# An SSM convolution beside a mixer MLP: half of the taps transposed by DMA, weights placed in halves, output sums by DMA, a new order

## The chip, the cores and the metric

The kernel runs on one core of a Trainium2 chip. A core has five engines that run their own instruction streams and meet through semaphores: TensorE (PE) for matmuls, VectorE (DVE) for elementwise work, ScalarE (ACT) for activations and for moving PSUM to SBUF, GpSimd (POOL), and SyncE (SP), which here only issues DMAs. PSUM is used as four pairs of banks. The metric is the device time of one execution in microseconds.

## The reference

The input `x` (called `A_q`) has 2048 tokens of 640 features. Two branches are mixed by a gate per token.

```python
g = sigmoid((x * gate_w).sum(-1))
# branch a: causal depthwise conv of k (4 taps), times v, long convolution, times q
kv = k_shift * v
y  = irfft(rfft(kv_pad) * rfft(ssm_k_pad))[:2048] + kv * ssm_D
a  = q * y                                  # q is x
# branch b: token mixing and an MLP
h  = gelu(layernorm(x) @ w1)                # 640 x 640
x1 = x + shift_tokens(h) @ w2               # four feature groups shifted by 1,-1,2,-2
b  = x1 + gelu(layernorm(x1) @ w3) @ w4     # 640 -> 1536 -> 640
out = g * a + (1 - g) * b
```

## The kernel before

Token `t` sits at partition p of half c with t = 1024 c + 8 p + rho, so that work goes by rho = 0 to 7 and c = 0, 1. One large SBUF arena holds every tensor at fixed offsets; pieces are used again for other tensors when they are free.

**Branch b.** LN1 takes statistics of each row (`bn_group`, L800 and L802 on DVE), a power of -0.5 on POOL (`ln_finish`, L794), and normalizes on DVE (`normal`, L626, tag xn). PE transposes the rows (L839), ACT copies them to `XT` (L652, tag xTe). `mm1` (L876) makes h; its 160-column groups leave a fifth tile whose rows travel by small DMAs on POOL's queue (L916, tag tail) to their shifted places in `HT`. mm2 (L983) adds onto x, which ACT has put into PSUM first (`seed`, L966). LN2 comes from sums that ACT accumulates (the eviction's accumulator and a Square pass, L638); its normalized rows go through a DMA transpose on SP's queue (L1006, tag xT). mm3 (L1026) and mm4 (L1044) are the MLP, in four stages of 512 tokens each. The weights w3 and w4 are loaded on POOL's queue once the places of w1, w2 and of the kv scratch are free.

**Branch a.** The convolution is done by transforms as matmuls over 128 frequencies, in two halves of 320 features each. `kv` is computed on DVE in four blocks (L621). The taps `ssm_k` arrive with features on partitions and must be transposed: 80 transposes on PE (L773) and eight evictions on ACT (L779) fill `TAP`, whose first row then gets ssm_D added on DVE. `forward` (L1075) makes the spectra of the taps ("h") and of kv ("k") for a half, which ACT evicts into slots; `unit` (butterfly, window, pointwise, fold) is all DVE; `inverse` (L1198) brings the product back, ACT scales it by the gate, DVE multiplies by q and adds onto the scaled b in `X` (tag fin), and SP's queue writes the output (L1227).

**The gate.** The gate weights are loaded as a column (L711); PE multiplies them with `XT` (L933), the result is corrected by LN1's statistics, and ACT makes tanh of it.

**Order.** Nothing is ordered by the source text. Every operation is a node with its reads and writes; a planner (`_forward`) plays the program with estimated costs and due times and emits each engine's instructions in the order in which it started them. Ties go by a table of ranks (`PRIO`). So a queue is strictly in order: an instruction that waits holds all that stand behind it, and this includes the DMA issues on SP and POOL. `FILL` groups of small matmuls (L717) with no use but to keep PE busy are put wherever the planner finds PE idle.

The core of the tap transposes before:

```python
SSM[:, c, 1024 * a + rho:1024 * a + 1024:8], ident))   # 5 per t, 16 t
o = TAP[:, :, 2 * m:2 * m + 2, :].rearrange("p h t d -> p t h d")
```

Of the kernel before, what the change touches and what calls it, by code (L numbers as in the profile page):

```python
# [88 lines left out]
class Prog:  # L89
# [82 lines left out]
    def dma(self, queue, fn, r=(), w=(), nbytes=0, cost=0.4, kind="dma", group=None, final=False, tag="", land=None):  # L172
# [27 lines left out]
    def _forward(self):  # L200
# [38 lines left out]
        while left:  # L239
# [42 lines left out]
            if n.array:  # L282
# [5 lines left out]
                if not warm:  # L288
                    cost += n.array
# [4 lines left out]
            free[e] = t + cost  # L294
            if n.kind == "c":
                n.end = t + cost
            elif n.kind == "dma":
                link = max(link, t + 1.2) + n.bytes / self.RATE
                n.end = link + n.land
            elif n.kind == "acc":  # L300
                alink = max(alink, t + 1.2) + n.bytes / 150e3
                n.end = alink + 1.6
            elif n.kind == "side":
                slink = max(slink, t + 1.0) + 0.2
                n.end = slink + (4.0 if link > t else 1.0)
            else:
                xlink = max(xlink, t + 1.0, link) + 1.2
                n.end = xlink + 0.5
# [114 lines left out]
def _bf16_bits(a):  # L423
# [5 lines left out]
FILL = 35  # L429
KV_DMA = ()  # L430
PW_DMA = ()
LN1_GROUPS = ((0,), (1,), (2, 3), (4, 5), (6, 7))
SPLIT = (0,)
LN2_DVE = ()
LN2_ACT = (1, 2, 3)
LN1_ACT = ()
INV = (0, 4, 2, 6, 1, 5, 3, 7)
FIN2 = (0,)
# [72 lines left out]
def bass_gated_mix__ssm_conv_h3__mixer_s_mlp__prompt_kernel(  # L511
# [55 lines left out]
    w3v = V(oW12, 7680).rearrange("p (c f) -> p c f", c=5)  # L567
    w4v = V(oW4, 7680).rearrange("p (c f) -> p c f", c=12)
# [9 lines left out]
    SSM = V(oS + 3 * SLOT, 10240).rearrange("p (c t) -> p c t", c=5)  # L578
    SHK = V(oGM + 1024, 2560).rearrange("p (j d) -> p j d", j=4)
    SHKROW = AR[0:1, oHT:oHT + 2560]  # L580
# [4 lines left out]
    DROW = AR[0:1, oS + 14080:oS + 14720]  # L585
# [93 lines left out]
    for sc in range(4):  # L679
        P.stage = sc  # L680
# [596 lines left out]
```

## Time and profile before

| what | value |
|---|---|
| median of three runs | 236.53 us (236.1 to 236.62) |
| the profiled execution | 235.83 us |
| its span, first to last instruction | 234.0 us |
| PE busy | 226.6 us (97%), 1689 matmuls |
| DVE busy | 217.2 us (93%) |
| ACT busy | 175.6 us (75%) |
| POOL busy | 29.0 us (12%) |
| DMA | 27.69 MB, mean 118 GB/s |
| mean granted TensorE clock | 0.993 |

A busy PE is not PE at its peak, since matmuls overlap: a matmul of 320 columns is listed with about 0.30 us, while 96 of them follow each other in 13.2 us. How often a line ran and how far apart its instructions start tells more than its busy time. In a timeline, a row gives start, length, engine, line, operation, count, and in brackets the idle time before it and what ended that. Where two instructions overlap, the lengths of a row and of its neighbour overlap too.

### The profile page before, as it was taken

What the parts mean: (1) busy time and instruction counts of PE and PEld (TensorE: products, weight loads), DVE (VectorE), ACT (ScalarE), POOL (GpSimd) and SP (SyncE); (2) the same over time, 40 slices, a digit from 0 to 9 for tenths busy, and PEclk for the clock granted to TensorE, in tenths of its full rate; (3) what the DMA queues carried; (4) which work ended last, traced back from release to release, by engine and by line L of the source; (5) the groups of instructions that cost most, each with busy time, mean ns of one, the idle gap of its engine ahead of it and who ended that gap; (6) DMA issues with size and microseconds to landing.
All of it is one profiled execution on the core that took longest, in us unless ns stands there. A gap on an engine that the chain in (4) does not pass through costs nothing.

```text
span 234.0 us, 4160 instructions
## 1 busy us (share of the span) xinstructions
PE 226.6 (97%) x1689; PEld 147.4 (63%) x1689; DVE 217.2 (93%) x277; ACT 175.6 (75%) x287; POOL 29.0 (12%) x38
## 2 busy tenths in 40 slices
PE   7999998997999998999999998999999999999998
PEld 7799565554677755446764454457755764577777
DVE  3994799999999969998998999999999999999995
ACT  2458998999899999899959869889237224662683
POOL 1312530304003420005203000000000000000000
PEclk9889999999999999999999999999999999999999
DMA  7999999201005997000426500008008010001055
GB/s 222 385 408 315 349 398 331 74 0 27 0 0 192 344 339 95 0 0 3 84 44 102 112 0 0 3 9 216 3 0 224 3 56 0 0 3 56 0 172 169
DMA packets 26484, 27.69 MB, mean 118 GB/s; under 512 B 12657, under 2 KB 22258, under 8 KB 26338
## 3 DMA queue, kind: packets, MB, share of 16 engines
q1 hardware_dynamic: 24674, 21.57, 31.7%
q0 software_dynamic: 1648, 5.54, 6.9%
q10 hardware_dynamic: 144, 0.33, 0.7%
q8 instruction: 13, 0.21, 0.4%
q14 instruction: 5, 0.04, 0.1%
HBM read 21.66 MB, written 2.62 MB: 104 GB/s over the span
## 4 chain that ended last, share of the span: by engine, by line
PE 42%; ACT 18%; DVE 18%; SPq 7%; issue 6%; DMA 5%; POOL 2%; POOLq 1%; ACTq 0%; DVEq 0%
DVE arena L621 18%; PE PS L1044 17%; ACT arena L652 14%; PE PS L1026 9%; PE PS L1198 7%; SPq L664 7%; DMA arena<-in_A_k_dram 5%; PE PS L1075 3%; ACT PS L966 3%; POOL arena L794 2%; PE PS L983 2%; PE PS L717 2%; PE PS L876 1%; ACT arena L638 1%; POOLq L1247 1%
## 5 line engine op out<-in xcount | busy, mean ns | idle before, releaser
L621 DVE TENSOR_TENSOR arena<-arena 128x2560 bf16<-128x2560 bf16 (+5 forms) x181 | 193.4, 1127 | 4.0 <-DMA arena<-in_A_k_dram 1.6
L652 ACT ACTIVATE arena<-PS 128x640 bf16<-128x640 f32 (+5 forms) x136 | 97.8, 799 | 25.8 <-PE PS L1026 13.1
L1026 PE MATMUL PS<-arena 128*128 128x512 bf16 x240 | 52.8, 379 | 0.7 <-DMA arena<-arena 0.7
L1044 PE MATMUL PS<-arena 128*128 128x320 bf16 x384 | 52.8, 299 | 0.0
L1044 PEld LDWEIGHTS PS<-arena 128*128 128x128 bf16 x384 | 37.5, 98 | 14.9 <-issue 0.3
L652 ACT ACTIVATE arena<-PS,arena 128x320 bf16<-128x320 f32 (+1 forms) x48 | 27.9, 618 | 25.1 <-PE PS L1044 23.2
L1026 PEld LDWEIGHTS PS<-arena 128*128 128x128 bf16 x240 | 23.3, 98 | 28.4 <-issue 0.9
L1075 PE MATMUL PS<-arena 128*128 128x320 bf16 x224 | 34.2, 300 | 1.6 <-ACT arena L652 1.5
L1075 PEld LDWEIGHTS PS<-arena 128*128 128x128 bf16 x224 | 20.0, 98 | 14.7 <-ACT arena L652 6.2
L638 ACT ACTIVATE arena<-arena 128x640 bf16<-128x640 bf16 (+2 forms) x30 | 22.8, 786 | 2.8 <-DVE arena L824 2.7
L876 PE MATMUL PS<-arena 128*128 128x512 bf16 (+1 forms) x125 | 23.3, 337 | 0.4 <-ACT arena L779 0.2
L983 PE MATMUL PS<-arena 128*128 128x320 bf16 x160 | 22.2, 299 | 1.4 <-issue 1.4
L966 ACT ACTIVATE PS<-arena 128x640 f32<-128x640 bf16 x32 | 22.3, 718 | 0.1
L983 PEld LDWEIGHTS PS<-arena 128*128 128x128 bf16 x160 | 15.6, 98 | 7.7 <-issue 1.7
L794 POOL TENSOR_TENSOR arena<-arena 128x4 f32<-128x4 f32 (+1 forms) x9 | 13.6, 1514 | 54.0 <-DVE arena L621 37.9
L800 DVE BATCH_NORM_STATS2 arena<-arena 128x6 f32<-128x320 bf16 x32 | 13.7, 462 | 4.5 <-DMA arena<-in_A_q_dram 4.5
L1198 PE MATMUL PS<-arena 128*128 128x320 bf16 x128 | 17.9, 299 | 0.0
L876 PEld LDWEIGHTS PS<-arena 128*128 128x128 bf16 x125 | 11.7, 98 | 8.9 <-ACT arena L779 0.5
L717 PE MATMUL PS<-arena 128*128 128x128 bf16 x175 | 14.3, 256 | 1.5 <-DVE arena L674 1.5
L1198 PEld LDWEIGHTS PS<-arena 128*128 128x128 bf16 x128 | 12.5, 98 | 5.0
L717 PEld LDWEIGHTS PS<-arena 128*128 128x128 bf16 x175 | 13.4, 119 | 2.3 <-DVE arena L674 1.5
L626 DVE TENSOR_SCALAR arena<-arena 128x640 bf16<-128x640 bf16 (+3 forms) x35 | 10.3, 320 | 2.8 <-POOL arena L794 2.1
(31 smaller groups left out, 69.4 us busy)
## 6 DMA issues: line engine op xcount, KB each, us to landing
arena<-in_B_w_dram POOLq DMA_DIRECT2D x4, 960.0 KB, 8.1
arena<-in_A_v_dram SPq DMA_DIRECT2D x4, 640.0 KB, 13.5
arena<-in_A_ssm_k_dram SPq DMA_DIRECT2D x5, 512.0 KB, 11.4
arena<-in_A_k_dram SPq DMA_DIRECT2D x4, 640.0 KB, 16.2
arena<-in_A_q_dram SPq DMA_DIRECT2D x4, 640.0 KB, 4.9
out_dram<-arena SPq DMA_DIRECT2D x16, 160.0 KB, 2.0
arena<-in_A_q_dram SPq DMA_DIRECT2D x7, 320.0 KB, 7.8
arena<-cG POOLq DMA_DIRECT2D x1, 1024.0 KB, 5.0
```

Source lines behind the costliest of these rows:

```text
L621: return dve(lambda e: e.tensor_tensor(o, a, b, op), [a, b], [o], c_tt(n), tag=tag, **kw)
L638: node = P.op("act", lambda e, ps: e.activation(o, i, func, **kw), r=r, w=[o], cost=c_act(n, naps, acc is not None, psum=False), tag=tag, ...
L652: node = P.op("act", lambda e, ps: e.activation(ov, inner(ps), func, **kw), r=r, w=[o], cost=c_act(n, len(r), acc is not None), job=job, t ...
L717: P.pe([(lambda e, ps: e.matmul(bank(ps, 0, 128), ones, ones, start=True, stop=True)) for _ in range(5)], r=[ones], cols=128 * 5, tag="fil ...
L794: P.op("pool", lambda e, ps: e.tensor_tensor(r, v, hv, ALU.pow), r=[v, HALF], w=[r], cost=1.1, tag="ln")
L876: fns.append(lambda e, ps, b=b, c=c, lhsT=lhsT: e.matmul(bank(ps, b, 256 * n), lhsT, XT[:, c, r0:r0 + n, :], start=(c == 0), stop=(c == 4)))
L966: P.seed(job, lambda e, ps: e.activation(two(ps, 320), x, ACTF.Copy), [X[:, c, rho, :]], c_act(640, psum=False), tag)
L983: fns.append(lambda e, ps, hh=hh, ft=ft, lhsT=lhsT: e.matmul(bank(ps, hh, 320), lhsT, w2v[:, ft, 320 * hh:320 * hh + 320], start=False, st ...
L1026: fns.append(lambda e, ps, b=b, ft=ft, c=c, sc=sc: e.matmul(bank(ps, b, 512), w3v[:, c, 128 * ft:128 * ft + 128], XT[:, c, 2 * sc:2 * sc + ...
L1044: fns.append(lambda e, ps, hh=hh, ft=ft, lhsT=lhsT: e.matmul(bank(ps, hh, 320), lhsT, w4v[:, ft, 320 * hh:320 * hh + 320], start=False, st ...
L1075: fns.append(lambda e, ps, w=w, b=b, rhs=rhs, st=(first and n == 0), en=(n == len(ss) - 1): e.matmul(bank(ps, b, 320), w, rhs, start=st, s ...
L1198: fns.append(lambda e, ps, kap=kap, ri=ri, c=c, r=r, s=s, n=n: e.matmul(bank(ps, c, 320), GM[:, kap, ri, r, s, :], Qs[kap][:, r, ri, c, :] ...
```

## The change

- **Taps.** Only features 0 to 319 of `ssm_k` are loaded to SBUF and transposed on PE, in three groups (128, 128 and 64 features, 16 transposes each) with one eviction per group. Features 320 to 639 are transposed from DRAM by six DMA transposes on SP's queue. They come out with token blocks in another order, so each half of the tokens is written to a scratch tensor in DRAM (tW) and read back (tR). The transposes depend on all loads of SP's queue. ssm_D is added on POOL, once per half.
- **Weights.** w3 and w4 are kept in halves: w3's first in w1's place, its second and w4's first in the kv scratch, w4's second in w2's place. w4's second half and the table GM depend on the first four xT.
- **Gate.** The gate weights are loaded as one row and turned into a column by five one-column matmuls.
- **LN1.** x is loaded in other pieces; the statistics of rho 1 come from ACT (Copy and Square passes with accumulators). LN2 needs one operation less on small columns per group.
- **Output sums.** For the first half, DVE multiplies into q's slot and four accumulating DMAs on POOL's queue add it onto `X`. In the second half, the first two pairs of rho are multiplied and added together.
- **Order.** The planner's costs are changed (bytes of loads, lands of DMAs, cost of POOL's power), fills are 60 single matmuls in place of 35 groups of five, and the ranks in `PRIO` are new.

```diff
-    SSM = V(oS + 3 * SLOT, 10240).rearrange("p (c t) -> p c t", c=5)
+    SSM = V(oS + 3 * SLOT, 6144).rearrange("p (c t) -> p c t", c=3)
...
-    for c in range(5):
-        load("sp", SSM[:, c, :], A_ssm_k[128 * c:128 * c + 128, :], 128 * 4096, tag="ssm")
...
-    P.dma("sp", lambda e, ps: e.dma_start(GWT, gate_w.rearrange("(c p) -> p c", p=128), allow_slow_non_contiguous=True),
-          w=[GWT], nbytes=400000, tag="gw")
+    load("sp", GROW, gate_w.rearrange("(o n) -> o n", o=1), 1280, tag="gw")
...
+    for c in range(3):
+        P.stage = c
+        n = 128 if c < 2 else 64
+        fns = [(lambda e, ps, c=c, n=n, t=t: e.transpose(
+            half16(ps)[:, n * t:n * t + n], SSM[0:n, c, 1024 * (t // 8) + t % 8:1024 * (t // 8) + 1024:8],
+            ident[0:n, 0:n])) for t in range(16)]
...
+        o = TAP[:, 0, :, 128 * c:128 * c + n]
+        evict(job, o, lambda ps, n=n: half16(ps)[:, 0:16 * n].rearrange("p (t d) -> p t d", t=16), ACTF.Copy, 16 * n,
+              tag="tap")
+
+    def add_d(h):
+        t0row = TAP[0:1, h, 0, :]
+        P.op("pool", lambda e, ps: e.tensor_tensor(t0row, t0row, DROW[h], ALU.add), r=[t0row, DROW[h]], w=[t0row],
+             cost=2.0, tag="ssmD")
...
+    back = nc.dram_tensor("taps1", (2048, 320), BF16).ap()
+    loads = [n for n in P.nodes if n.eng == "sp" and n.kind == "dma"]
+    for a in range(2):
+        P.stage = a
+        o = TAP[:, 1, 8 * a:8 * a + 8, :]
+        for d in (0, 128, 256):
+            n = min(128, 320 - d)
+            P.dma("sp", lambda e, ps, o=o[:, :, d:d + n], i=A_ssm_k[320 + d:320 + d + n, 1024 * a:1024 * a + 1024]:
+                  e.dma_start_transpose(o, i), w=[o[:, :, d:d + n]], nbytes=2048 * n, cost=1.3, kind="xpose", tag="tT").deps.update(loads)
+        if a == 0:
+            add_d(1)
+        half = back[1024 * a:1024 * a + 1024, :]
+        out_ = P.dma("sp", lambda e, ps, o=o, half=half: e.dma_start(half.rearrange("(q p) d -> p q d", p=128), o),
+                     r=[o], nbytes=900000, tag="tW")
+        in_ = P.dma("sp", lambda e, ps, o=o, half=half: e.dma_start(o, half.rearrange("(p r) d -> p r d", r=8)),
+                    w=[o], nbytes=700000, tag="tR")
+        in_.deps.add(out_)
...
-    w3v = V(oW12, 7680).rearrange("p (c f) -> p c f", c=5)
-    w4v = V(oW4, 7680).rearrange("p (c f) -> p c f", c=12)
+    w3h = [V(o, 3840).rearrange("p (c f) -> p c f", c=5) for o in (oW12, oW4)]
+    w4h = [V(o, 3840).rearrange("p (c f) -> p c f", c=6) for o in (oW4 + 3840, oW12 + 3840)]
...
-            tt(g2, g2, Qh[:, :, sel, :], ALU.mult, n, tag="fin")
-            tt(xs, xs, g2, ALU.add, n, tag="fin")
+            if half in FIN_DMA:
+                qs = Qh[:, :, sel, :]
+                tt(qs, g2, qs, ALU.mult, n, tag="fin")
+                P.dma("pool", lambda e, ps, xs=xs, qs=qs: e.dma_start(xs, qs, accum_op=ALU.add), r=[xs, qs], w=[xs],
+                      nbytes=256 * n, cost=0.9, kind="acc", tag="fina")
+            else:
+                tt(g2, g2, Qh[:, :, sel, :], ALU.mult, n, tag="fin")
+                tt(xs, xs, g2, ALU.add, n, tag="fin")
...
-FILL = 35
+FILL = 60
+FILLN = 1
...
+LN1_STAT = (1,)
...
-FIN2 = (0,)
+FIN2 = {0: 4, 1: 2}
+FIN_DMA = (0,)
```

More of the change, by code (lines that the diff above doesn't have):

```diff
@@ L170, in pe, with dma @@
         return job
-    def dma(self, queue, fn, r=(), w=(), nbytes=0, cost=0.4, kind="dma", group=None, final=False, tag="", land=None):
+    def dma(self, queue, fn, r=(), w=(), nbytes=0, cost=0.46, kind="dma", group=None, final=False, tag="", land=None):
         node = self._new(queue, [fn], cost, kind, r, w, group, tag)
@@ L287, in _forward @@
                     duty, carry = carry, 0.0
[L288 removed]
+                if not warm or n.tag == "fill":
                     cost += n.array
@@ L294, in _forward @@
             free[e] = t + cost
+            if n.kind == "xpose":
+                free[e] = max(free[e], link - 1.5)
             if n.kind == "c":
@@ L710, in bass_gated_mix__ssm_conv_h3__mixer_s_mlp__prompt_kernel @@
-    load("sp", DROW, A_ssm_D.rearrange("(o n) -> o n", o=1), 1280, tag="ssm")
-    P.dma("sp", lambda e, ps: e.dma_start(GWT, gate_w.rearrange("(c p) -> p c", p=128), allow_slow_non_contiguous=True),
-          w=[GWT], nbytes=400000, tag="gw")
-    for _ in range(FILL):
-        P.pe([(lambda e, ps: e.matmul(bank(ps, 0, 128), ones, ones, start=True, stop=True)) for _ in range(5)], r=[ones],
-             cols=128 * 5, tag="fill", bits=(False, None))
+        load("sp", w2v[32 * j:32 * j + 32, 4, :], B_w2[160 * j + 128:160 * j + 160, :], 88000, tag="w2", group="w2t")
@@ new lines, in bass_gated_mix__ssm_conv_h3__mixer_s_mlp__prompt_kernel @@
+    for _ in range(FILL):
+        P.pe([(lambda e, ps: e.matmul(bank(ps, 0, 128), ones, ones, start=True, stop=True)) for _ in range(FILLN)], r=[ones],
+             cols=128 * FILLN, tag="fill", bits=(False, None))
+    job = P.pe([(lambda e, ps, c=c: e.matmul(bank(ps, 0, 1, o=c), GROW[:, 128 * c:128 * c + 128], ones[0:1, 0:1],
+                                             start=True, stop=True)) for c in range(5)],
+               r=[GROW, ones], cols=5 * 56, tag="gwt", bits=(False, None))
+    evict(job, GWT, lambda ps: bank(ps, 0, 5), ACTF.Copy, 5, tag="gwt")
@@ new lines, in act_stats @@
+    def act_stats(rho):
+        rsl = slice(rho, rho + 1)
+        for c in range(2):
+            x = X[:, c, rho, :]
+            act(JUNK, x, ACTF.Copy, 640, scale=1.0 / D, acc=MV1[:, rho, 2 * c:2 * c + 1], accgroup=("m1", rho), tag="st")
+            act(JUNK, x, ACTF.Square, 640, scale=D ** -0.5, acc=MV1[:, rho, 2 * c + 1:2 * c + 2], accgroup=("m1", rho),
+                tag="st")
+        m, s, v = MV1[:, rsl, 0:4:2], MV1[:, rsl, 1:4:2], VAR1[:, rsl, 0:2]
+        dve(lambda e: e.scalar_tensor_tensor(out=v, in0=m, scalar=-1.0, in1=m, op0=ALU.mult, op1=ALU.mult),
+            [m], [v], 0.08, tag="ln")
+        dve(lambda e: e.scalar_tensor_tensor(out=v, in0=v, scalar=1e-5, in1=s, op0=ALU.add, op1=ALU.add),
+            [v, s], [v], 0.08, tag="ln")
+        ln_finish(VAR1, RS1, 0.75, rsl)
@@ L1209, in inverse @@
                 evict(job, o, lambda ps, c=c: bank(ps, c, 320), ACTF.Copy, 320, scale=GG[:, gi:gi + 1], tag="gy")
-            pair = rho // 4 == 1 and half in FIN2
-            if half in FIN2 and not pair:
+            paired = INV.index(rho) // 2 < FIN2[half]
+            pair = rho // 4 == 1 and paired
+            if paired and not pair:
                 continue
```

127 lines of the change are left out of this document (68 added, 59 removed), and 50 rows, old and new, of the table PRIO.

## The prediction

> **What bounds the kernel now.** I read the page first, then the timelines of TensorE (PE) and VectorE (DVE), the chain of waits, and the groups by shape.
>
> ```profile
> span 234.0 us, 4160 instructions
> ...
> PE 226.6 (97%) x1689; PEld 147.4 (63%) x1689; DVE 217.2 (93%) x277; ACT 175.6 (75%) x287; POOL 29.0 (12%) x38
> ...
> GB/s 222 385 408 315 349 398 331 74 0 27 0 0 192 344 339 95 0 0 3 84 44 102 112 0 0 3 9 216 3 0 224 3 56 0 0 3 56 0 172 169
> ```
>
> PE and DVE are both near full, so a change pays only if it moves a point at which one of them stood still, or takes work from both. The timelines (start, length, engine, line, what, count, idle time before) give those points.
>
> ```profile
> 12.06 1.27 PE L839 MATMUL PS<-arena 128*128 128x128 bf16 x10
> ...
> 14.91 4.53 PE L876 MATMUL PS<-arena 128*128 128x256 bf16 x40
> ...
> 21.49 2.70 PE L773 MATMUL PS<-arena 128*128 128x128 bf16 x40
> ...
> 35.73 0.72 PE L839 MATMUL PS<-arena 128*128 128x128 bf16 x10 [0.89 <-DVE arena L626]
> ...
> 43.26 2.33 PE L876 MATMUL PS<-arena 128*128 128x512 bf16 x10 [0.21 <-ACT arena L779]
> ...
> 58.73 19.18 PE L983 MATMUL PS<-arena 128*128 128x320 bf16 x140 [1.41 <-issue]
> ...
> 77.88 1.14 PE L933 MATMUL PS<-arena 128*128 128x1 bf16 x40
> 79.39 3.73 PE L1075 MATMUL PS<-arena 128*128 128x320 bf16 x24 [0.38 <-ACT arena L652]
> ...
> 92.44 13.11 PE L1026 MATMUL PS<-arena 128*128 128x512 bf16 x60 [0.72 <-DMA arena<-arena]
> ...
> 217.37 12.12 PE L1198 MATMUL PS<-arena 128*128 128x320 bf16 x88
> 229.32 3.79 PE L717 MATMUL PS<-arena 128*128 128x128 bf16 x65
> ```
>
> ```profile
> 29.24 4.23 DVE L621 TENSOR_TENSOR arena<-arena 128x5120 bf16<-128x5120 bf16 x2 [1.57 <-DMA arena<-in_A_k_dram]
> ...
> 83.63 1.51 DVE L626 TENSOR_SCALAR arena<-arena 128x640 bf16<-128x640 bf16 x4 [0.93 <-POOL arena L794]
> ...
> 86.83 4.49 DVE L621 TENSOR_TENSOR arena<-arena 128x1280 bf16<-128x1280 bf16 x5 [0.88 <-ACT arena L652]
> ...
> 221.80 9.77 DVE L621 TENSOR_TENSOR arena<-arena 128x1280 bf16<-128x1280 bf16 x18 [0.33 <-ACT arena L652]
> ```
>
> DVE waits for k until 29.24, then computes kv. PE needs all of kv before the k transforms (L1075) at 79.39. DVE can start window and pointwise (86.83) only behind them. From 92.44, the first mm3, PE runs almost without a gap to its last inverse matmul at 217.37 + 12.12 = 229.5; DVE ends at 221.80 + 9.77 = 231.6, the last output follows, and the span closes at 234.0. Between the last inverse matmul and the close lie 4.5 us. The 65 fills at 229.32 run beside that tail. So the end is set by when PE reaches mm3, plus 137.1 us of saturated PE (229.5 - 92.44).
>
> The profiled execution took 235.83 us: 1.8 around the span of 234.0. The median of the three runs is 236.53, 0.7 above it; I work with the span and add 2.5.
>
> **Loads and kv.** In the chain of waits, the first block of k is the load that the start waits for:
>
> ```profile
> 17.45 11.66 DMA arena<-in_A_k_dram
> ```
>
> Ahead of and with it, before: x 2.62 MB, v 0.66, w1 0.82, ssm_k 2.62, halo 0.49, w2 0.82, k 0.66, in all 8.68 MB. After: x 2.62, w1 0.82, ssm_k 1.31 (320 rows only), two v 1.31, half of the table cF 0.52, halo 0.49, k 0.66: 7.73 MB. At the 315 to 408 GB/s of the third to sixth slice of the GB/s row, taken as 364, 0.95 MB less is 2.6 us: kv starts at 26.6. The last x moves from behind 7.2 MB to behind about 4.2, so LN1 starves less. The other bound is no gain: xn for rho 7 needs a buffer that PE's transposes of rho 5 free, and it stands ahead of kv in DVE's order.
>
> ```profile
> L621 DVE TENSOR_TENSOR arena<-arena 128x2560 bf16<-128x2560 bf16 x78 | 112.6, 1485 | 0.3
> ...
> L621 DVE TENSOR_TENSOR arena<-arena 128x1280 bf16<-128x1280 bf16 x68 | 52.0, 819 | 1.5 <-ACT arena L652 1.2
> ...
> L621 DVE TENSOR_TENSOR arena<-arena 128x5120 bf16<-128x5120 bf16 x8 | 22.6, 2820 | 1.6 <-DMA arena<-in_A_k_dram 1.6
> ...
> L621 DVE TENSOR_TENSOR arena<-arena 128x640 bf16<-128x640 bf16 x16 | 7.6, 490 | 0.6
> ...
> L621 DVE TENSOR_TENSOR arena<-arena 128x4 f32<-128x4 f32 x8 | 1.2, 156 | 0.0
> ...
> L621 DVE TENSOR_TENSOR arena<-arena 1x640 bf16<-1x640 bf16 x1 | 0.5, 473 | 0.0
> ```
>
> kv is 8 of 2.82 and 16 of 1.49, 46.4 us, with one xn and some small ones 47.4: it ends at 74.0 at the latest, where PE could not use it before 79.39.
>
> **The taps.** Eight ACT evictions and 80 PE transposes become three evictions of 2048, 2048 and 1024 columns and 48 transposes.
>
> ```profile
> L638 ACT ACTIVATE arena<-arena 128x640 bf16<-128x640 bf16 x28 | 22.3, 825 | 2.8 <-DVE arena L824 2.7
> ...
> L779 ACT ACTIVATE arena<-PS 128x1280 bf16<-128x1280 bf16 x8 | 9.4, 1284 | 0.0
> ```
>
> ACT loses 9.4 and pays, per column, 5120/1280 x 1.28 / 1 = 5.1: 4.3 us less. It matters because ACT is full there:
>
> ```profile
> 30.00:40.00 10.00, 9.11 (x81) 5.74 (x79) 10.00 (x11) 9.34 (x10) 2.33 (x4) 1.00 1.05 374
> 40.00:50.00 10.00, 9.79 (x78) 6.40 (x75) 9.90 (x8) 9.88 (x16) 2.11 (x4) 1.00 0.22 73
> ```
>
> PE sheds 32 transposes, at 2.70 for 40 (the row at 21.49) 2.2 us. The other half of the taps goes through six DMA transposes from DRAM, two writes to DRAM and two reads, behind all loads. Nothing in this profile shows a transpose from DRAM. The nearest rows are those of xT, 163,840 B each, and a 640 KB load:
>
> ```profile
> L1006 SPq DMA_TRANSPOSE arena<-arena x16: 1200/1276/1836, 84.2 to 132.1; - x16
> ...
> DMA to landing us min/median/max: 2.6/2.7/6.3
> ```
>
> ```profile
> arena<-in_B_w_dram POOLq DMA_DIRECT2D x4, 960.0 KB, 8.1
> ...
> arena<-in_A_q_dram SPq DMA_DIRECT2D x4, 640.0 KB, 4.9
> ```
>
> By size a 262 KB transpose takes 1.6 x 1.28 = 2.04 us of SP's queue. All loads end near 39.5: before, the GB/s row falls off in its eighth slice, at about 43, and 1.3 MB less is 3.6 us. Then 6 x 2.04 = 12.2, a landing of 4.3, a write and a read of 4.9 each: 66. PE first reads these taps behind mm3's first 60 matmuls, near 99. So I cost them at nothing, but they hold SP's queue: all 16 xT stand behind them, the first needed at about 77, which leaves 11 us. GpSimd (POOL) has the same order: the pow of LN2's first group now stands behind w3's first half (it waits for mm1's end), the D add (waits for three of the transposes), w3's second half (waits for kv) and w4's first. I take each transpose as 2.04; the range of it, from 1.3 (no growth with size) to several times that, is the slower rival.
>
> **LN1 and the gate.** rho 1's statistics leave DVE (four bn_stats, two aggregates) for four ACT passes at the start, where ACT waited for PE in any case; four passes of 0.83 (row L638) cost 3.3 there and should end before the shk evictions. The gate weights as a row cost five one-column matmuls instead of 640 tiny elements; 40 of the 80 gate matmuls move ahead into mm1, 1.1 us (the row at 77.88). The x loads' smaller pieces let the first transposes start about 1.2 us sooner than 12.06. The planner's new costs move nothing by themselves; only the order counts.
>
> **mm2 and the k transforms.** Before, the 140 mm2 ended at 58.73 + 19.18 = 77.9. To take off: 2.2 of transposes, 2.5 of stalls behind ACT and the tails of HT (1.41 at 58.73, 0.89 at 35.73, 0.21 at 43.26), 1.2 of earlier start. To add: 1.1 of gate matmuls. mm2 ends at 73.2. Four transforms (0.5) and 40 gate matmuls (1.1) come next, so the k transforms start at 74.8, with kv ready at 74.0: 4.6 earlier. From there to mm3 it took 13.05 (92.44 - 79.39), with 40 gate matmuls (1.1) and five fills (0.3), which are gone: 11.6. mm3 starts at 86.4, 6.0 earlier. xT must be in by then. The pow ahead of it, next to DVE's tensor_tensor, took
>
> ```profile
> 106.74 2.94 POOL L794 TENSOR_TENSOR arena<-arena 128x4 f32<-128x4 f32 x1 [23.14 <-DVE arena L621]
> ```
>
> 2.94. w3's second half may go when kv's last read of its scratch ends, two TT ahead of 74.0, at 71.0; two issues of 0.86 and the pow end at 75.6. DVE comes to the four xn two TT behind kv, at 77.0. The transposes issue from 77.4; four take 5.1, and a landing of 2.7 makes 85.2: just in time. With the 6.3 that was the longest before, mm3 starts at 88.8.
>
> **From mm3 to the end.** PE has the same 137.1 us. DVE sheds, behind 86.83: half 0's four output sums (4 x 0.82), half 1's first two pairs merged (4 x (2 x 0.49 - 0.82) = 0.65) and three LN operations on four columns (0.16 each): 4.4; the D add (0.47, now on POOL) went out of the kv stage already. DVE began at 86.83 and ended at 231.6, 144.8; it begins 4.6 earlier, at 82.2, and needs 140.4, ending at 222.6, while PE's end at 223.5 plus the old 2.1 asks for 225.6. DVE has 3 us to spare: its saving is worth nothing by itself, but keeps it from becoming the bound. The sums go to four DMAs of 327 KB on POOL's queue, which no row shows with an accumulate. Bounds: a plain 640 KB load, 4.9, or the weights' 8.1 for 960 KB. The last is issued about 7 us ahead of DVE's end, and SP's outputs queue behind it; at 4.9 it is hidden, at 8.1 it costs 1 to 2.
>
> ```profile
> L664 POOL DMA_DIRECT2D arena<-in_B_w_dram x4: 831/858/883, 73.9 to 79.1; - x4
> ```
>
> These issues ran beside DVE's saturated stretch and took 0.86. [...]
>
> **Sum.** 234.0 - 6.0 = 228.0 of span; 229.8 for the profiled execution; 230.5 against the median.
>
> **Rivals.** (1) The clock. The granted clock (column PEclk) before:
>
> ```profile
> 8.00:10.00 2.00, 2.00 (x9) 0.98 1.09 373
> 10.00:12.00 2.00, 2.00 (x21) 0.50 1.04 397
> 13.00:14.00 1.00, 1.00 (x18) 0.82 1.03 414
> 14.00:15.00 1.00, 1.00 (x21) 1.00 1.06 414
> ```
>
> It fell to 0.50 for 3.4 us behind the one-row shk matmuls, and 35 fills beside the first transposes brought it back. Only 12 fills stand there now, with waits between. If the clock comes back one window of 3.4 us later, mm1 loses 1.7; if two, 3.4, and kv's start waits with it through the xn buffers: 230.5 + 3.4 = 233.9. [...]
>
> (2) mm3 waits for xT or the accumulating DMAs run late: about 2.4 of the gain goes, 232.9. For it: xT arrives at 85.2 against 86.4, and w3's second and w4's first half are in flight then. Against it: the tables GM and w4's second half now wait for the first four xT.
>
> (3) The other side, slower. A transpose from DRAM holds SP far longer than 2.04. Point: xT is late without cost until (77 - 39.5 - 14.1) / 6 = 3.9 us each, and the whole gain is gone at (83.0 - 39.5 - 14.1) / 6 = 4.9. At 6.5 each the chain ends at 92.6, 15.6 late, and the time is 230.5 + 15.6 = 246. For it: the source has 2 KB runs in DRAM and no row shows such a transfer. Against it: xT's 16 have a steady median of 1.28.
>
> **How the numbers follow.** The forecast 0.58, own range 226.5 to 232.5 (low end: kv at 72, its instructions overlapping a little, lets the k transforms start 2.8 earlier, and PE's last stalls go); rival 1 0.15; rival 2 0.07; rival 3 0.20, of which 0.03 falls near its break-even, within 0.2% (0.5 us, about what a measurement can tell here) of 236.5. Faster 0.80, same 0.03, slower 0.17. The range 226.5 to 237 leaves out what is beyond 237 in rival 3 and a little below.
>
> **What the profile after would show.** Right: kv's first TT near 26.6; k transforms near 74.8; mm3 near 86.4, with 137 behind it; ACT's tap evictions 5 us; all six transposes landed by 55 and the first xT issued near 77. Wrong: clock 0.50 beyond 13.4; SP still in the taps at 77; POOL's pow waiting for the D add; a gap in PE ahead of mm3 or of the first transforms that read the new taps; the last output waiting for an accumulate.
>
> ```profile
> DMA to landing us min/median/max: 1.9/2.0/4.3
> ```
>
> The tail is right if the last output lands 2.0 after its issue and its issue follows DVE's last sum.

## The result, and the profile after

The changed kernel takes 232.69 us (median of four executions, 231.94 to 233.19), the kernel before 236.57 beside it: a ratio of 0.984 (95% interval 0.981 to 0.987). The forecast was 230.5. The profiled execution took 231.94 us, the fastest of the four; its span is 229.9 us. In the experiments below a few executions (one of e3, four of f4, one of g1) lie more than 1.5% above the fastest of their kernel; the ratios leave these out, the medians and ranges hold all. The page of the profiled execution has these rows:

```profile
span 229.9 us, 3896 instructions
...
PE 218.2 (95%) x1536; PEld 139.2 (61%) x1547; DVE 213.2 (93%) x260; ACT 173.9 (76%) x291; POOL 39.8 (17%) x44
...
GB/s 165 333 399 330 340 341 337 113 156 312 167 187 0 324 135 215 141 30 29 82 106 103 0 3 0 0 3 0 0 230 226 3 0 117 0 0 52 80 211 231
```

The first two slices of the GB/s row moved less than before (222 and 385). The timelines of PE and then of DVE, with the points that the prediction named:

```profile
33.15 0.72 PE L890 MATMUL PS<-arena 128*128 128x128 bf16 x10 [0.73 <-ACT arena L661]
...
51.13 22.09 PE L1038 MATMUL PS<-arena 128*128 128x320 bf16 x160
...
76.22 3.75 PE L1141 MATMUL PS<-arena 128*128 128x320 bf16 x24 [1.15 <-DVE arena L630]
...
86.98 12.89 PE L1092 MATMUL PS<-arena 128*128 128x512 bf16 x58 [0.18 <-issue]
...
210.71 13.20 PE L1264 MATMUL PS<-arena 128*128 128x320 bf16 x96
```

```profile
28.42 4.23 DVE L630 TENSOR_TENSOR arena<-arena 128x5120 bf16<-128x5120 bf16 x2 [0.63 <-DMA arena<-in_A_k_dram]
32.56 0.44 DVE L635 TENSOR_SCALAR arena<-arena 128x640 bf16<-128x640 bf16 x1
...
220.58 5.40 DVE L630 TENSOR_TENSOR arena<-arena 128x1280 bf16<-128x1280 bf16 x10 [0.39 <-ACT arena L661]
```

kv starts at 28.42, only 0.8 us earlier than before. mm2 (L1038) ends at 73.2, and PE then waits 1.15 us for kv, which it did not do before. mm3 starts at 86.98, 5.46 earlier. PE's last inverse matmul ends at 223.9, 136.9 us later, but the span closes 6.0 us behind that instead of 4.5. So 4.1 us of the span are gone: 5.5 ahead of mm3, less 1.4 behind it.

SP's timeline shows the new taps, and two lines' own views the accumulating DMAs (L1292) and the outputs (L1300):

```profile
43.39 6.72 SPq L812 DMA_TRANSPOSE arena<-in_A_ssm_k_dram  x5
...
65.05 0.32 SPq L818 DMA_DIRECT2D arena<-taps  x1
79.49 5.16 SPq L1065 DMA_TRANSPOSE arena<-arena  x4
```

```profile
L1292 POOL DMA_DIRECT2D arena<-arena x4: 1255/1276/1349, 187.9 to 218.1; - x4
...
DMA to landing us min/median/max: 4.5/5.0/5.8
```

```profile
L1300 SPq DMA_DIRECT2D out_dram<-arena x16: 372/497/1197, 192.5 to 226.8; - x16
...
DMA to landing us min/median/max: 1.9/2.9/3.9
```

The last read of the taps is issued at 65.05 and lands some 5 us later; xT follows at 79.49, and mm3 waits only 0.18. The outputs now land 2.9 us after their issue, before 2.0.

### The profile page after: what moved, and what is told of

The parts are those of the page before. It is cut to its first block, busy times and chain, and to the rows that moved or that the text cites. A ratio compares the mean times of both kernels' runs of the same rounds, so it can differ in the third digit from the quotient of the medians.

```text
span 229.9 us, 3896 instructions
## 1 busy us (share of the span) xinstructions
PE 218.2 (95%) x1536; PEld 139.2 (61%) x1547; DVE 213.2 (93%) x260; ACT 173.9 (76%) x291; POOL 39.8 (17%) x44
## 4 chain that ended last, share of the span: by engine, by line
PE 54%; DVE 23%; ACT 8%; DMA 7%; SPq 4%; issue 1%; DVEq 0%
PE PS L1110 23%; DVE arena L630 23%; PE PS L1092 20%; DMA arena<-in_A_k_dram 7%; ACT arena L661 7%; PE PS L1141 6%; PE PS L1264 6%; SPq L673 4%; ACT arena L647 2%; DVE arena L635 0%; DVEq L409 0%; DVE arena L869 0%; DVEq L411 0%
## 5 line engine op out<-in xcount | busy, mean ns | idle before, releaser
L630 DVE TENSOR_TENSOR arena<-arena 128x2560 bf16<-128x2560 bf16 (+5 forms) x168 | 190.2, 1189 | 3.8 <-ACT arena L661 1.5
L661 ACT ACTIVATE arena<-PS 128x640 bf16<-128x640 f32 (+7 forms) x140 | 102.7, 823 | 23.1 <-PE PS L1092 14.4
L1092 PE MATMUL PS<-arena 128*128 128x512 bf16 x233 | 51.6, 379 | 0.9 <-issue 0.4
L1110 PEld LDWEIGHTS PS<-arena 128*128 128x128 bf16 x384 | 37.5, 98 | 14.9 <-issue 0.3
L1092 PEld LDWEIGHTS PS<-arena 128*128 128x128 bf16 x240 | 23.3, 98 | 28.3 <-ACT arena L661 0.6
L1141 PEld LDWEIGHTS PS<-arena 128*128 128x128 bf16 x224 | 19.7, 98 | 15.2 <-ACT arena L661 6.4
L647 ACT ACTIVATE arena<-arena 128x640 bf16<-128x640 bf16 (+2 forms) x34 | 26.3, 792 | 1.8 <-DMA arena<-in_A_q_dram 1.2
L1292 POOL DMA_DIRECT2D arena<-arena x4 | 5.2, 1289 | 100.2 <-DVE arena L630 80.6
L1038 PE MATMUL PS<-arena 128*128 128x320 bf16 x160 | 22.1, 299 | 0.0
L831 POOL TENSOR_TENSOR arena<-arena 128x4 f32<-128x4 f32 (+1 forms) x9 | 15.5, 1724 | 29.2 <-DVE arena L635 21.8
L1038 PEld LDWEIGHTS PS<-arena 128*128 128x128 bf16 x160 | 15.6, 98 | 6.5 <-ACT PS L1020 0.4
L930 PEld LDWEIGHTS PS<-arena 128*128 128x128 bf16 x125 | 12.0, 99 | 8.2 <-ACT arena L661 0.2
L1264 PEld LDWEIGHTS PS<-arena 128*128 128x128 bf16 x128 | 12.5, 98 | 5.2
L851 DVE BATCH_NORM_STATS2 arena<-arena 128x6 f32<-128x320 bf16 x28 | 12.2, 472 | 3.2 <-DMA arena<-in_A_q_dram 3.2
L635 DVE TENSOR_SCALAR arena<-arena 128x640 bf16<-128x640 bf16 (+3 forms) x31 | 9.7, 355 | 2.6 <-PE PS L890 1.3
L970 POOL DMA_DIRECT2D arena<-arena x18 | 9.7, 543 | 14.2 <-ACT arena L661 14.2
```

Source lines behind the costliest of these rows:

```text
L630: return dve(lambda e: e.tensor_tensor(o, a, b, op), [a, b], [o], c_tt(n), tag=tag, **kw)
L647: node = P.op("act", lambda e, ps: e.activation(o, i, func, **kw), r=r, w=[o], cost=c_act(n, naps, acc is not None, psum=False), tag=tag, ...
L661: node = P.op("act", lambda e, ps: e.activation(ov, inner(ps), func, **kw), r=r, w=[o], cost=c_act(n, len(r), acc is not None), job=job, t ...
L831: P.op("pool", lambda e, ps: e.tensor_tensor(r, v, hv, ALU.pow), r=[v, HALF], w=[r], cost=cost, tag="ln")
L851: dve(lambda e, o=o, x=x: e.bn_stats(o, x), [x], [o], 0.393, tag="bn", group=("bn", id(mv), rho, c))
L930: fns.append(lambda e, ps, b=b, c=c, lhsT=lhsT: e.matmul(bank(ps, b, 256 * n), lhsT, XT[:, c, r0:r0 + n, :], start=(c == 0), stop=(c == 4)))
```

## The experiments

All start from the changed kernel with its instruction order written out as a list, so that only the named edit moves. Each was run beside the kernel before; ratios are to that kernel, with 95% intervals. First the table of what the traces show, in us: the first kv product, the last transposes of LN1 (L890), the transforms of k, mm3, PE's last inverse matmul (its end), and the span.

| run | kv | L890 | k transforms | mm3 | inverse end | span |
|---|---|---|---|---|---|---|
| before | 29.24 | 35.73 | 79.39 | 92.44 | 229.49 | 234.0 |
| after | 28.42 | 33.15 | 76.22 | 86.98 | 223.91 | 229.9 |
| f1 after, same order | 29.57 | 34.31 | 77.37 | 88.14 | 225.07 | 230.7 |
| e1 sums on DVE | 29.76 | 34.49 | 78.19 | 89.11 | 228.04 | 234.1 |
| e2 no sums | 29.32 | 34.06 | 77.76 | 88.69 | 225.82 | 230.5 |
| e3 k first | 27.66 | 32.38 | 77.18 | 89.74 | 226.88 | 232.4 |
| e4 kv short | 29.30 | 34.03 | 76.05 | 86.98 | 224.12 | 230.0 |
| f2 xn 7 first | 30.40 | 33.74 | 78.00 | 89.82 | 226.75 | 232.3 |
| f3 more fills | 30.19 | 34.92 | 77.99 | 90.03 | 226.96 | 232.5 |
| f4 taps on PE | 28.56 | 33.29 | 81.58 | 92.73 | 229.67 | 236.0 |
| g1 ssm_k 128 rows | 27.83 | 32.56 | 75.63 | 87.67 | 224.59 | 230.1 |
| g2 x in pairs | 28.40 | 33.13 | 76.20 | 88.48 | 225.41 | 231.0 |
| h1 rows and fills | 28.99 | 33.72 | 76.79 | 87.34 | 224.48 | 230.0 |
| h2 combined | 27.29 | 32.01 | 75.07 | 85.62 | 222.76 | 228.3 |

**The changed kernel again, as a baseline (f1).** No edit but the written order.

> The changed kernel itself, with its instruction order written out as a list; a baseline for the three runs beside it. It should repeat 232.7 us (231.9 to 233.2 in four executions). If the scatter comes from when k lands, its executions should spread over more than 1 us and go with the mean clock: .98 near 232, .97 near 233.

Measured: 232.66 us (231.87 to 234.19), ratio 0.981 [0.975, 0.986]. The median repeats. The scatter does not go with the mean granted clock as I had written (232.8 at .984, 231.87 at .985). In its profile k landed 1.15 us later, and everything behind it, up to the last inverse matmul, is later by about the same amount:

```profile
29.57 4.23 DVE L630 TENSOR_TENSOR arena<-arena 128x5120 bf16<-128x5120 bf16 x2 [1.71 <-DMA arena<-in_A_k_dram]
33.72 0.44 DVE L635 TENSOR_SCALAR arena<-arena 128x640 bf16<-128x640 bf16 x1
```

```profile
34.31 0.72 PE L890 MATMUL PS<-arena 128*128 128x128 bf16 x10 [2.07 <-DVE arena L635]
...
77.37 3.75 PE L1141 MATMUL PS<-arena 128*128 128x320 bf16 x24 [1.15 <-DVE arena L630]
...
88.14 12.89 PE L1092 MATMUL PS<-arena 128*128 128x512 bf16 x58 [0.18 <-issue]
```

In both profiles L890 comes 4.73 us after kv's start, the transforms of k 47.80 after it, mm3 58.56. PE hangs on the landing of k twice: through kv itself, and through the last normalization of LN1 (L635), which stands behind the first two kv products in DVE's queue. (The row of L890 after the change names an eviction of ACT instead; it ended at 33.14, the normalization at 33.00. The last transposes of LN1 lie 4.72 to 4.74 us behind kv's start in every run of the table from after to h2 but f2, which moves this normalization.) That is why PE's wait for kv is 1.15 us in both: when k is late, mm1 and mm2 are late too.

**The output sums (e1, e2).** e1 puts the four sums back on DVE, e2 leaves them out.

```diff
-P.dma("pool", lambda e, ps, xs=xs, qs=qs: e.dma_start(xs, qs, accum_op=ALU.add), r=[xs, qs], w=[xs], ...)
+tt(xs, xs, qs, ALU.add, n, tag="fina")    # e1: two behind their multiplications, two behind DVE's last fold
+pass                                      # e2
```

> The changed kernel with the same order of instructions on every engine; only the four accumulating DMAs of half 0's output sums are DVE additions again, the first two right behind their multiplications, the last two behind the last fold. Theory T (the accumulating DMAs fill the DMA engines in the last 12 us, and twelve outputs queue behind them: 1.5 us of tail): the twelve outputs issue earlier, the DMA share at 218 to 222 falls from 1.2 to below 0.6, the way from PE's last inverse matmul to the close falls from 6.0 to about 4.5, but DVE works 3.3 us more, of which some 1.5 reach the end because DVE's folds feed the last inverse matmuls; time 232.0 to 233.5. Rival U (the tail is long only because outputs come in a bunch): the tail stays at 6.0 and DVE's 1.5 to 3.3 come on top: 234 to 236.

> The changed kernel in the same order, with the four accumulating DMAs left out and nothing in their place: the first 320 features of the output lack the SSM branch. It prices these DMAs alone. Theory T: 1.5 us less than the changed kernel, 231.2, and a tail of 4.5 us behind PE's last matmul. Rival U: within 0.4 us of the changed kernel, 232.7.

Measured: e1 235.09 us (233.96 to 236.0), ratio 0.993 [0.990, 0.996]; e2 231.51 (229.69 to 233.1), ratio 0.977 [0.972, 0.981]. DVE and PE at the end of e1:

```profile
199.46 31.61 DVE L630 TENSOR_TENSOR arena<-arena 128x2560 bf16<-128x2560 bf16 x34
```

```profile
219.16 8.88 PE L1264 MATMUL PS<-arena 128*128 128x320 bf16 x64 [1.60 <-DVE arena L630]
```

At the end of e1 DVE has no gap any more, and PE waits for it. From mm3 to the close it is 145.0 us in e1 (234.1 - 89.11), 141.8 in e2 (230.5 - 88.69) and 142.9 after. Four adds of 0.82 us cost 3.2 us there, all of their length; as DMAs they cost 1.1 (0.6 to 1.5, since the profiles with them go from 142.4 to 143.3). So U was right on DVE, at these places of the adds. For the DMAs theory T holds in e2: the way from PE's last inverse matmul to the close is 4.7 us there. In e1 that way stayed at 6.1, because DVE ended 3.0 us behind PE, so e1 says nothing of the DMAs' price. Where the 1.1 goes shows in the windows from 218 to 222 us, first of after, then of e2 (busy time of PE, PEld, DVE, ACT and POOL, granted clock, DMA share, GB/s):

```profile
218.00:220.00 2.00, 2.00 (x17) 1.43 (x16) 1.97 (x3) 1.72 (x4) 1.25 (x1) 1.00 1.21 146
220.00:222.00 2.00, 2.00 (x17) 1.43 (x16) 1.57 (x3) 1.72 (x5) 0.00 (x0) 1.00 1.24 150
```

```profile
218.00:220.00 2.00, 2.00 (x17) 1.42 (x16) 2.00 (x4) 1.72 (x5) 0.00 (x0) 1.00 0.00 0
220.00:222.00 2.00, 2.00 (x17) 1.43 (x15) 1.96 (x3) 1.72 (x5) 0.00 (x0) 1.00 0.03 8
```

The last two accumulating DMAs fill the DMA engines (share 1.2) at 150 GB/s just when the outputs begin; behind them the outputs queue. The outputs land 2.0 us after their issue in e1 and e2, 2.9 after; the last one is issued 0.8 us behind the end of DVE after (226.77 for 225.98), 0.1 in e2 (227.97 for 227.90).

Both profiles lost time ahead of mm3, too: mm3 comes 59.4 us behind kv's start, and PE no longer waits for kv. The cause is a stretch of 3.4 us at half clock behind the wait for L890: from L890 to the point where PE could start the transforms of k it is 43.6 us in e1 and 41.9 in f1, 1.7 more. The row and the window are e1's, the second window is f1's, where a wait of 2.07 us had no such effect:

```profile
34.49 0.74 PE L890 MATMUL PS<-arena 128*128 128x128 bf16 x10 [2.23 <-DVE arena L635]
```

```profile
36.00:38.00 2.00, 2.00 (x10) 1.11 (x8) 1.97 (x2) 1.10 (x2) 0.00 (x0) 0.50 1.05 385
```

```profile
36.00:38.00 2.00, 2.00 (x12) 1.03 (x11) 1.97 (x2) 2.00 (x4) 0.00 (x0) 1.00 1.02 392
```

**k first, and a shorter kv (e3, e4).** e3 changes the order on SP; e4 leaves out one addition of kv.

```diff
-sp: v:1, FM:0, kh:0, kh:0, D, D, v:0, k:0
+sp: kh:0, kh:0, k:0, v:1, FM:0, D, D, v:0                       # e3
-                tt(TA, TA, TB, ALU.add, 5120, tag="kv")
+                if h == 0:                                       # e4
+                    tt(TA, TA, TB, ALU.add, 5120, tag="kv")
```

> The changed kernel with one thing moved: on SP's queue the halo and the first block of k are issued ahead of the second ssm_k group's followers (first v, first half of cF, second v). Theory K (the start of kv is what PE's k transforms wait for, 1.15 us; at the start k's landing costs 0.63): k lands near 24, kv starts at 27.8 where the normalization that stands ahead of it on DVE ends, 0.6 earlier, and the time falls by 0.6 to 232.1. Rival C (PE's half clock until 16 us is what holds the early part): no change, 232.7.

> The changed kernel in the same order without one DVE addition of 5120 columns (2.8 us) in the last kv block: that block leaves out taps 2 and 3 of the short convolution, so its output is another. Theory K: PE's wait of 1.15 us ahead of the k transforms goes, they start at 75.1 and the time falls by 1.1 to 1.2, to 231.5; of the 2.8 us the rest buys nothing, since PE then comes last. Rival C (PE itself bounds this place) : less than 0.3 us.

Measured: e3 234.17 us (231.22 to 234.81), ratio 0.986 [0.981, 0.990]; e4 231.93 (231.24 to 234.32), ratio 0.981 [0.977, 0.985]. e3 is slower than either theory had it. In e3 kv started at 27.66 and mm2 ended 0.8 us earlier than after, but DVE then stood still for k's second block, and PE waited longer:

```profile
41.26 23.95 DVE L630 TENSOR_TENSOR arena<-arena 128x5120 bf16<-128x5120 bf16 x12 [1.45 <-DMA arena<-in_A_k_dram]
```

```profile
77.18 12.59 PE L1141 MATMUL PS<-arena 128*128 128x320 bf16 x68 [2.89 <-DVE arena L630]
```

With that wait the granted clock fell to 0.50 from about 76.4 to 83.2 us (worked out from the windows' mean clock), and the transforms took 12.59 us instead of 10.8. In e4 PE did not wait for kv, and mm3 came 57.7 us after kv's start instead of 58.6: of the 2.3 us by which kv is shorter (45.5 for 47.7), 0.9 arrive, since PE's own chain is ready only that much earlier. K was right that kv sets the point and wrong on how much there is to have. (The time of e4 is too near to f1's 232.66 to tell them apart, so this rests on the profile.)

**The normalization ahead of kv (f2).**

```diff
-dve: kv:0, kv:0, xn:7, kv:0
+dve: xn:7, kv:0, kv:0, kv:0
```

> The last normalization of LN1 (xn of rho 7, c 1) goes ahead of the first two kv products on DVE. Theory Q (a queue): those two products wait for k and hold the normalization behind them, PE waits for it (0.73 us in the changed kernel's profile, 2.0 to 2.2 in two of the experiments) and the longer waits bring a second stretch at clock .50 near 35 to 39 us. Then that wait goes, no execution has a half clock between 30 and 45 us, and the median falls by 0.5 to 1.0 us, to 231.7 to 232.2, with a spread below 1 us; PE waits up to 1.9 us for kv before the transforms of k. Rival K (kv is the bound, wherever PE's gap lies): no change within 0.4 us, 232.3 to 233.0.

Measured: 233.15 us (232.57 to 234.36), ratio 0.983 [0.978, 0.988]. PE's wait near 33 is gone (L890 follows mm1 at once at 33.74), and the time is no better. PE comes sooner to its wait for kv, which is now 2.34, and the clock falls to 0.50 for 3.4 us behind it. Theory Q falls; K fits, although the time lies 0.15 above its range: one of the two ties is cut, the other holds.

**Fills at the start (f3).**

```diff
-FILL = 60
+FILL = 104
-pe: fill, shk, shk, shk, shk
+pe: fill, fill x12, shk, fill x8, shk, fill x8, shk, fill x8, shk, fill x8
```

> 44 more fill matmuls between 6 and 11 us, where PE has gaps; no other work is moved. Theory C (the early gaps bring the half clock from 8.6 to 16): the clock stays at 1.00 until 10 us or later and is half for one window of 3.4 us in place of two; mean clock .99; the work behind it starts about 1 to 1.7 us earlier, 231.0 to 231.9. Theory K (k and kv set the time): no change within 0.4 us. If fills only delay, up to 1 us slower.

Measured: 234.32 us (233.57 to 234.9), ratio 0.987 [0.983, 0.992]; 1.7 above the baseline, more than any of the three expectations. The clock did more than theory C wanted: it was 1.00 in every window of f3 up to 42 us. The window of after, then that of f3:

```profile
12.00:14.00 2.00, 2.00 (x22) 2.00 (x21) 1.39 (x7) 1.05 (x1) 1.25 (x2) 0.50 1.03 394
```

```profile
12.00:14.00 2.00, 2.00 (x33) 1.86 (x32) 2.00 (x7) 1.05 (x2) 0.94 (x1) 1.00 1.03 395
```

But mm1 started at 16.64 instead of 15.64 (f1): the fills between the shk jobs took longer than the gaps. And kv waited 1.18 us for k, which landed at 30.19, later than in f1 (29.57). So the longer half clock after the change is real, and a full clock alone does not bring kv forward. Whether the half clock costs anything was not shown, since these fills cost time themselves and k was late.

**Taps back on PE (f4).** Five groups of 128 features on PE, no tT, tW, tR; the two added loads of ssm_k stand behind w2, the two added groups between mm1's jobs.

```diff
-    SSM = V(oS + 3 * SLOT, 6144).rearrange("p (c t) -> p c t", c=3)
+    SSM = V(oS + 3 * SLOT, 10240).rearrange("p (c t) -> p c t", c=5)
...
-    for c in range(3):
+    for c in range(5):
```

> One part undone: all 640 features of ssm_k are loaded and transposed on PE (five groups of 128 features), evicted by ACT; no DMA transposes, no tW and tR. All else as in the changed kernel, the two added groups stand between mm1's jobs near 34 us. The prediction's account: PE gets back 2.3 us of transposes (1.15 us for 16) and ACT some 4.5 us of evictions, both ahead of mm2; mm2 ends 2.3 to 4.5 later than 73.2, less the 1.15 us that PE waited for kv: mm3 starts 1.2 to 3.4 later and the time is 233.9 to 236. Rival: the gain of the change came from the loads and the order, and ACT and PE had room there: 232.4 to 233.2.

Measured: 240.69 us (237.64 to 242.42), ratio 1.010 [1.005, 1.015]: 7 to 8 us more than the baseline, outside what I wrote. Its profile is of one of the fastest executions (237.84) and shows 5.3 us of span:

```profile
37.51 1.26 PE L1128 MATMUL PS<-arena 128*128 128x320 bf16 x8 [1.97 <-ACT arena L661]
38.60 1.14 PE L786 MATMUL PS<-arena 128*128 128x128 bf16 x16
41.94 2.11 PE L917 MATMUL PS<-arena 128*128 128x512 bf16 x9 [2.20 <-ACT arena L661]
...
92.73 12.89 PE L1079 MATMUL PS<-arena 128*128 128x512 bf16 x58 [0.18 <-issue]
```

PE stands 4.2 us behind the two evictions of 2048 columns, and DVE 2.1 us at 42.82 for k's second block behind the added loads. mm3 comes 64.2 us after kv's start. So with this part undone in this order, the rest of the change gains nothing. The places of the added work are mine and not a planner's, and the added loads delay k's second block, so the amount is an upper bound of what this part is worth.

**The rate of the loads (g1, g2).**

```diff
-        load("sp", SSM[0:n, c, :], A_ssm_k[128 * c:128 * c + n, :], 4400 * n, tag="ssm")
+        load("sp", SSM[0:128, c, :], A_ssm_k[128 * c:128 * c + 128, :], 4400 * 128, tag="ssm")    # g1
-X_LOADS = ((0, 1), (1, 2), (2, 4), (4, 6), (6, 8))
+X_LOADS = ((0, 2), (2, 4), (4, 6), (6, 8))                                                        # g2
```

> One load changed: the third load of ssm_k, 64 rows in the changed kernel, brings 128 rows (262 KB more, of which nothing is used). Theory R (the loads' rate): after the 64-row load the next ones run below the full rate (188 to 303 GB/s at 8 to 10 us in seven profiles of kernels that have it, 382 in the one that loads 128 rows there), so k lands late. Then 8 to 10 us shows 370 GB/s or more and the first kv product starts no later than in the changed kernel (28.4 to 29.6) in spite of 0.7 us more of bytes: 27.7 to 28.7; time 231.5 to 232.5. Rival B (bytes alone count): the rate at 8 to 10 us stays at 190 to 300 GB/s and kv starts 0.7 us later; 233.0 to 233.6.

> x of rho 0 and 1 is loaded in one piece of 2560 bytes per row for each c, as before the change, in place of two of 1280 bytes. Theory R: the 1280-byte pieces run at 128 to 178 GB/s between 3.7 and 5.2 us, where the kernel before moved 376 to 430; then bytes moved by 6 us rise by 0.2 to 0.3 MB, k lands 0.5 to 0.8 us earlier, and the time falls by as much where k holds kv: 231.7 to 232.4. Against it: LN1's first statistics start 0.3 us later. Rival: the small pieces bring the first row group sooner and that is worth more: 232.7 to 233.5.

Measured: g1 233.26 us (230.91 to 234.72), ratio 0.982 [0.976, 0.988]; g2 232.11 (231.37 to 233.04), ratio 0.978 [0.973, 0.983]. The windows from 8 to 10 us, f1 first, then g1:

```profile
8.00:10.00 2.00, 1.63 (x10) 0.57 (x7) 2.00 (x10) 2.00 (x4) 0.14 (x1) 0.59 1.01 261
```

```profile
8.00:10.00 2.00, 2.00 (x16) 1.06 (x15) 2.00 (x12) 2.00 (x4) 0.59 (x1) 0.53 1.02 371
```

The rate went as theory R said, and kv started at 27.83, earlier than in both profiles of the changed kernel in spite of the 262 KB more. (In h1 below, with the same load, the rate was 326 and kv started at 28.99, so the rate is shown and the start is one profile. The added rows take up what the higher rate brings: without their 0.26 MB, g1 has moved 8.73 MB by 28 us and h1 8.41, against 8.74 after and 8.55 in f1.) The DMA share is as full in both windows (1.01 and 1.02), at 261 GB/s with the load of 64 rows and at 371 with 128; why the same share moves less is not shown. g2 moved 410 GB/s from 4 to 6 us against f1's 237, but only 225 from 6 to 8 us against 303, and 8.74 MB by 28 us, as after. Its kv start, 28.40, lies at the edge of the baseline's range and its time inside it: the rate is shown, a gain is not. g1's median did not follow its kv start either; it lies in rival B's range. In its profile the clock fell behind the wait for kv, a gap of 1.17 us as in f1 (1.15):

```profile
78.00:80.00 2.00, 2.00 (x10) 1.12 (x9) 2.00 (x6) 1.27 (x3) 0.01 (x1) 0.55 1.03 365
```

mm3 came at 87.67 instead of 27.83 + 58.56 = 86.4.

**Fills in the wait for kv (h1), and all together (h2).** h1 is g1 with 16 fills ahead of the transforms of k. h2 has g1's and g2's edits, e3's order with k's second block ahead of the fourth, and 12 fills.

```diff
-FILL = 60
+FILL = 76                                  # h1; 72 in h2
-pe: gate:3, fwdk:0
+pe: gate:3, fill x16, fwdk:0
-sp: FM:1, k:3, k:1                         # h2
+sp: FM:1, k:1, k:3
```

> The run with 128 rows in the third load of ssm_k, and beside it 16 fill matmuls (0.06 us each) ahead of the transforms of k, where PE waits 1.15 to 2.9 us for kv in every profile so far. Theory W (the wait sets off the clock): that wait is followed by a stretch at clock .50 from about 76 to 80 us in five of the nine profiles that show it, and it costs 1 to 2 us; with the fills the clock stays at 1.00 there, the transforms of k take 10.8 us in place of 11.9, and with kv from 27.8 mm3 starts at 86.4: 231.0 to 231.8 us, with a smaller scatter than 230.9 to 234.7. Rival: 0.2 us of work left in the gap is not what sets it off (or fills delay the transforms): 232.8 to 233.6 as without them.

> Four repairs of the loads and the wait together: 128 rows in the third load of ssm_k, x of rho 0 and 1 in one piece, k's first block ahead of v's, and k's second block ahead of the fourth (the experiment with k first had a 1.45 us wait for it), with 12 fills ahead of the transforms of k. kv then starts when DVE ends LN1, about 27.0, and runs 45.8 us without a wait; k's transforms start at 74.8, mm3 at 85.6, and 142.9 us later is the end: span 228.5, 230.4 us (229.8 to 231.2). Rival: the loads' sum binds and a later block waits instead (v or k's third): 231.5 to 233.

Measured: h1 231.84 us (231.35 to 233.44), ratio 0.977 [0.974, 0.981]; h2 230.88 (230.34 to 231.63), ratio 0.973 [0.970, 0.976]. (The expectation of h1 miscounts: PE waits for kv in seven of the profiles up to there, and in five of these, e3, f2, f3, g1 and g2, the clock falls.) h1's window where g1's clock was 0.55, and its PE:

```profile
78.00:80.00 2.00, 1.95 (x15) 1.10 (x12) 2.00 (x4) 2.00 (x5) 1.17 (x1) 1.00 1.03 374
```

```profile
75.66 1.07 PE L730 MATMUL PS<-arena 128*128 128x128 bf16 x16
76.79 3.75 PE L1141 MATMUL PS<-arena 128*128 128x320 bf16 x24
...
87.34 13.11 PE L1092 MATMUL PS<-arena 128*128 128x512 bf16 x60
```

The fills lie in the gap and delay nothing; mm3 comes 58.35 us after kv's start. In this profile kv started late again (28.99), so h1 shows the clock repaired, not the load. The evidence is thin: without fills the clock stayed at 1.00 behind such a gap in two profiles of five, with them in both profiles there are (h1, h2), and the intervals of h1 and g1 overlap. h2's DVE and PE:

```profile
27.29 4.21 DVE L630 TENSOR_TENSOR arena<-arena 128x5120 bf16<-128x5120 bf16 x2
```

```profile
75.07 3.75 PE L1141 MATMUL PS<-arena 128*128 128x320 bf16 x24 [0.29 <-DVE arena L630]
...
85.62 13.11 PE L1092 MATMUL PS<-arena 128*128 128x512 bf16 x60
```

kv no longer waits for k, and mm3 lies where it was expected (85.6), as does the span of 228.3. h2 computes the whole reference and is faster than both kernels: 6.4 us below the 237.31 beside it, and its slowest execution (231.63) is below the fastest of the changed kernel (231.87). By 10 us it has moved 2.84 MB, against 2.26 after and 2.87 before: with the third load at 128 rows and x in pairs together, the rate of the kernel before is back. What each of its edits brings alone is not taken apart.

## Why the prediction was right, point by point

- **The sign and the size:** the sign is right. Of the 6.0 us, 3.9 came in the median and 4.1 in the span. 232.69 lies inside the whole range but 0.2 outside the forecast's own one (226.5 to 232.5), next to the 232.9 of rival 2, of which the accumulating DMAs came about in part and the wait of mm3 for xT did not. The parts on weights, gate, LN1 and order were not run alone.
- **kv starts at 26.6: failed.** It is the largest miss ahead of mm3, 1.8 us. The rate of 364 GB/s was taken from the middle of the old GB/s row. Up to 28 us the windows add up to 8.74 MB after, 9.41 before; 0.67 MB at 364 GB/s is the 1.8 us. Nearly all of the 0.67 is missing between 4 and 10 us (0.66), where the narrow pieces of x and the load of 64 rows run; g1 and g2 show that these shapes lower the rate there (261 GB/s for 371, 237 for 410), and h2 that the rate comes back without them. How much of the 1.8 each costs is not shown. And 1.8 is the smallest of it: in the seven profiles with these loads in this order (after, f1, e1, e2, e4, f2, f3) kv waited for k until 28.42 to 30.40. What spreads it stays open.
- **kv ends where PE could not use it yet; the k transforms start at 74.8 because PE comes then: failed.** mm2 ended at 73.2 as predicted, and PE would have come at 75.07, but kv sets the transforms, 47.80 us after its start in six profiles (after, f1, f3, g1, g2, h1). The prediction had 47.4 for this and missed the start. That mm2 came out to the tenth is in part luck: the first transposes started 0.4 us sooner (11.64 for 12.06), not 1.2, 0.73 us of the stalls are still there at 33.15, and in f1, where k was later, mm2 ended at 74.4.
- **From the k transforms to mm3 11.6:** 10.76. The part gained 0.8 more and covered over half of the miss, so that mm3 (86.98 for 86.4) looked nearly exact; that is luck, and in f1 mm3 is at 88.14.
- **The taps:** right. ACT and PE are relieved (ACT's three evictions of taps take 4.8 us for 5.1 forecast; f4 gives an upper bound of what hangs on it), and the chain of DMA transposes is hidden, though not as sized: 1.31 us of issue in the median (2.27 at most) against 2.04, but it began at 43.4 instead of 39.5 and ended near 70 instead of 66. The slow rival did not come.
- **From mm3 136.9 us of saturated PE:** right (137.1).
- **"DVE has 3 us to spare: its saving is worth nothing by itself": failed.** The profile with the sums back on DVE (e1) has DVE full and PE waiting for it; their 3.3 us reach the end as 3.2. The sentence went on that the saving keeps DVE from becoming the bound; that half is right.
- **The accumulating DMAs are hidden at a landing of 4.9: failed.** They land after 5.0 and cost about 1.1, since they hold the DMA engines (share 1.2) when the outputs begin. The price of 1 to 2 was given for 8.1. The tail has 6.0 instead of 4.5 (4.7 in e2, without them).
- **Rival 1, the clock:** the half clock did last 3.4 us longer, 6.8 us from about 9.3 to 16.1 (worked out from the windows' mean clock), but mm2 ended at 73.2 all the same; the 1.7 given for that did not show. That the fills bring the clock back was the author's estimate: in f4, with the same 12 fills there, the half clock lasted 3.4 us. The clock matters at two other places: behind the wait for kv (3.4 us at 0.50 in f2, f3, g1 and g2, 6.8 in e3), where the change had opened a gap that was not there before, and behind a late L890 (3.4 us in e1 and in e2).
- **Rival 2, xT:** just in time, 0.18 us, as written.

## What to carry to other kernels

Ask of each gap what two chains meet there, and look for the one event on which both hang: here PE hung twice on the landing of one load, so that moving either chain alone (f2, e4) brought little, and only moving the load and filling the wait (h2) brought 1.8 us against the baseline. When bytes are taken from the front of a load queue, take the rate from the first microseconds of the new shapes (partitions and bytes per row), not from the old mean: here 245 to 303 GB/s from 4 to 10 us, for the 364 taken. A short wait on PE can cost more than its length if the clock falls behind it (g1: a wait of 1.17 us, 3.4 us at 0.50, and mm3 1.3 us late); a handful of fills in the wait is cheap where the wait is sure (h1: 16 of them took 1.07 us of it and delayed nothing).

## What the runs showed of the hardware that was not expected

- A gap of 1.15 to 1.2 us on PE, with 1.3 us of one-column matmuls ahead of it, was followed by 3.4 us at clock 0.50 (worked out from the windows' mean clock) in three profiles (f3, g1, g2) and not in two others with the same gap (after, f1). The two longer gaps brought it too: 2.3 us (f2) 3.4 us of it, 2.9 us (e3) 6.8. What separates g2 (gap from 75.04) from after (gap from 75.07) stays open. One-column matmuls are not needed: behind matmuls of 512 columns, gaps of 2.23 us (e1) and 2.02 (e2) ahead of L890 brought 3.4 us at 0.50, and one of 2.07 (f1) did not.
- While a load of 64 rows of 4 KB runs, the queue moves less: 188 to 303 GB/s at 8 to 10 us in the nine profiles that have it, 326 to 382 in the four with 128 rows (f4, g1, h1, h2).
- Accumulating DMAs of 327 KB from SBUF to SBUF (after): 1.28 us to issue, 5.0 to land, 146 to 150 GB/s at a full DMA share while the last two are in flight.
- Transposes by DMA from DRAM (after), up to 262 KB each: 1.3 us to issue in the median, 2.9 to 7.6 to land.
